# First loads of a fused S5 and GELU-MLP kernel on one core: fewer x transposes, bulk loads in one queue, parameter rows in one transpose

## The chip, the cores and the metric

The kernel runs on one core of a Trainium2 chip. The metric is the device time of one execution in microseconds (us), lower is better. Executions of the same program are compared in rounds on the same chip. Each execution has a time, a span (from the first to the last instruction, 1.3 to 2 us less than the time) and a mean granted clock of TensorE (1.000 is full). An execution is called slow here when it is more than 1.5% above the fastest of its kernel. Verdicts use the others alone, the "fast" ones.

## The reference, cut to what matters

```python
x = A_x                                            # 1 x 2048 x 640, bf16
g = sigmoid((x * gate_w).sum(-1, keepdims=True))
Bu = einsum("bld,pd->blp", x, B_bar)               # complex; B_bar from B_re, B_im, Lambda, log_dt
for t in range(2048): h = Lam_bar * h + Bu[:, t]   # a linear recurrence per state, complex
a = 2 * einsum("blp,dp->bld", h_all, Cmat).real + x * Dskip
b = gelu(x @ w1 + b1) @ w2 + b2                    # 640 -> 1728 -> 640
out = g * a + (1 - g) * b
```

## The kernel before

The kernel cuts the 2048 rows into four tiles of 512. It needs x in two forms: transposed (`xT`, loaded by DMA transposes, which turn the matrix on its way in; 640 on partitions in five slabs of 128, for the matmuls) and natural (`xn`, for the gate and the skip term). TensorE does W1, then B_re and B_im, then W2 and C, tile after tile. VectorE does the recurrence as scans and builds its tables from the parameters first. ScalarE takes results out of PSUM, the memory into which TensorE writes its sums. A small list scheduler in the kernel orders each engine's work from priorities and assumed durations.

TensorE starts with tile 0. It works slab by slab, so that it can start with the first slab of xT and W1:

```python
xtrans(0, [0], 0, 1.27)                 # one DMA transpose for each slab, Sync queue
xtrans(0, [1], 1, 1.27)
w1load(0, "act", -101)
w1load(1, "sp", 2)
for k in range(2, KD):
    xtrans(0, [k], 2 * k - 1, 1.27)
    w1load(k, "sp", 2 * k)
load("w1_r", "sp", ...)                 # the remaining 704 columns of W1, 880 KB
...
for ci, src in enumerate((A_B_re, A_B_im)):
    load_T(f"B{ci}", ..., prio=30 + ci) # two DMA transposes of 640 x 640, Sync queue
xtrans(1, range(KD), 32, 3.4)
load("w2a", "sp", ...); load("w2b", "sp", ...)
xtrans(2, ...); C_re, C_im; xtrans(3, ...)
```

GpSimd's queue loads the rest, as soon as the first matmul on the last slab of W1 is done ("late"):

```python
m1_first()                              # W1, columns 0 to 1023, tile 0
load("b2",  "pool", ..., reads=["late"])
load("dsk", "pool", ..., A_Dskip.partition_broadcast(128), reads=["late"])
load("gwb", "pool", ..., gate_w.partition_broadcast(128), reads=["late"])
xnload(0, "g", ..., reads=["late"])     # natural x tile 0, 640 KB, GpSimd
m1(0, NW)                               # W1, the remaining columns
bproj(0)                                # B_re (25 matmuls), then B_im (25 matmuls)
...
xnload(1, "g", ..., reads=["late"])     # natural x tile 1, 640 KB, GpSimd
```

The parameters (Lambda_re, Lambda_im, log_dt and b1) are loaded as rows and turned into columns by four small TensorE transposes, each result copied by VectorE.

Of the kernel before, what the change touches and what calls it, by code (L numbers as in the profile page):

```python
# [8 lines left out]
FP32 = mybir.dt.float32  # L9
BF16 = mybir.dt.bfloat16  # L10
# [137 lines left out]
class Prog:  # L148
# [8 lines left out]
    def op(self, name, eng, dur, reads, writes, fn, prio=None, lat=0.0, after=()):  # L157
        deps = {}
        for k in reads:
            for w in self.last_w.get(k, ()):  # L160
                deps[w.idx] = w
        for k in writes:
            for w in self.last_w.get(k, ()):
                deps[w.idx] = w
            for r in self.last_r.get(k, ()):
                deps[r.idx] = r
        for a in after:
            deps[a.idx] = a
        deps = list(deps.values())
        E = self.E  # L170

        def run(eg, deps=deps, eng=eng, fn=fn):
            E.wait(eng, *[d.done for d in deps])
            return fn()

        it = self.sch.add(name, eng, dur, deps, run, prio=prio, lat=lat)
        for k in writes:
            self.last_w[k] = [it]
            self.last_r[k] = []
        for k in reads:  # L180
            self.last_r.setdefault(k, []).append(it)
        return it


def bass_gated_mix__ssm_conv_s5__dense_activation_gelu__prompt_kernel(
# [20 lines left out]
    F = B_w1.shape[1]  # L206
    assert S % 512 == 0 and D % 128 == 0 and P == D
    KD = D // 128
    KP = P // 128
# [4 lines left out]
    NF = (F + 127) // 128  # L214
    FL = F - (NF - 1) * 128
# [10 lines left out]
    with ExitStack() as es:  # L226

        def SB(name, shape, dt):
            return es.enter_context(nc.sbuf_tensor(name, list(shape), dt))

        xT = [SB(f"xT_{i}", [128, KD, 512], BF16) for i in range(NQ)]
        xn = [SB(f"xn_{i}", [128, 4, D], BF16) for i in range(2)]
# [4 lines left out]
        Gl = [SB(f"Gl_{i}", [128, NF, 512], BF16) for i in range(2)]  # L237
        dsk = SB("dsk", [128, D], BF16)
        gwb = SB("gwb", [128, D], BF16)
        b1col = SB("b1col", [128, NF], FP32)  # L240
        rows = SB("rows", [KP, 3, 128], BF16)
        b1rows = SB("b1rows", [NF, 128], BF16)
        lcol = SB("lcol", [128, 3, KP], FP32)
        dtb = SB("dtb", [128, KP], BF16)
        acol = SB("acol", [128, KP], FP32)
        thcol = SB("thcol", [128, KP], FP32)
# [5 lines left out]
        ident = SB("ident", [128, 128], BF16)  # L252
# [33 lines left out]
        PS = [es.enter_context(nc.psum_tensor(f"ps{i}", [128, 512], FP32)) for i in range(8)]  # L286
# [13 lines left out]
        op = pr.op  # L300

        def inc(eng, ins):
            return E.inc(eng, ins, eng + "_s")

        def dma_inc(eng, ins, sem):
            SEM(sem)
            E.count.setdefault(sem, 0)
            ins.then_inc(sems[sem], 16)
            E.count[sem] += 16
            return (sem, E.count[sem])  # L310
# [11 lines left out]
        def load(name, eng, sem, dst, src, writes, prio, dur=0.5, lat=2.5, reads=(), **kw):  # L322
            def fn():
                return dma_inc(eng, engines[eng].dma_start(dst, src), sem)  # L324
            return op(name, eng, dur, reads, writes, fn, prio=prio, lat=lat)

        def load_T(name, sem, pairs, writes, prio, dur, lat=3.0):
            def fn():
                t = None
                for dst, src in pairs:  # L330
                    t = dma_inc("sp", nc.sync.dma_start_transpose(dst, src), sem)  # L331
                return t
            return op(name, "sp", dur, (), writes, fn, prio=prio, lat=lat)

        def xnload(q, tag, prio=None, reads=()):
            load(f"xn{q}{tag}", "pool", f"l_xn{q}{tag}", xn[q % 2][:, :, :],
                 x2[q * 512:(q + 1) * 512, :].rearrange("(c p) d -> p c d", p=128),
                 [("xn", q % 2, 0), ("xn", q % 2, 1)], prio, dur=1.0, lat=6.0, reads=reads)

        NW = 8  # L340
        FW = NW * 128
        nmain = (NF - 1) * 128

        def xtrans(q, ks, prio, dur):
            load_T(f"xT{q}_{ks[0]}", f"l_xT{q}_{ks[0]}", [(xT[q][:, ks[0]:ks[-1] + 1, :], x2[q * 512:(q + 1) * 512, ks[0] * 128:(ks[-1] + 1) * 128])],
                   [("xT", q, k) for k in ks], prio, dur)

        def w1load(k, eng, prio):
            load(f"w1_{k}", eng, f"l_w1{k}", W1sb[:, k, 0:FW], B_w1[k * 128:(k + 1) * 128, 0:FW], [("w1", k)], prio=prio, lat=2.6)

        xtrans(0, [0], 0, 1.27)
        xtrans(0, [1], 1, 1.27)
        w1load(0, "act", -101)
        w1load(1, "sp", 2)
        for k in range(2, KD):
            xtrans(0, [k], 2 * k - 1, 1.27)
            w1load(k, "sp", 2 * k)
        load("w1_r", "sp", "l_w1r", W1sb[:, :, FW:F], B_w1[:, FW:F].rearrange("(k p) f -> p k f", p=128), [("w1", "r")], prio=20, lat=5.0)

        def f_b1z():  # L360
            return inc("pool", nc.gpsimd.memset(b1rows[:, :], 0.0))

        op("b1z", "pool", 0.2, (), ["b1a", "b1b0", "b1b1"], f_b1z, prio=-50)
        for i, (nm, src) in enumerate((("lre", A_Lambda_re), ("lim", A_Lambda_im), ("ldt", A_log_dt))):
            load(nm, "act", "l_" + nm, rows[:, i, :], src.rearrange("(k p) -> k p", p=128), [("rows", i)], prio=-100 + i, dur=0.45)
        load("b1a", "act", "l_b1a", b1rows[0:NF - 1, :], B_b1[0:nmain].rearrange("(j p) -> j p", p=128), ["b1a"], prio=-97, dur=0.4)
        for i in range(2):
            load(f"b1b{i}", "act", f"l_b1b{i}", b1rows[NF - 1:NF, 64 * i:64 * i + FL], B_b1[nmain:F].rearrange("(j p) -> j p", j=1), [f"b1b{i}"], prio=-96, dur=0.4)


        def f_iota():
            inc("pool", nc.gpsimd.iota(io_i[:, :], pattern=[[1, 128]], base=0, channel_multiplier=-1))
# [33 lines left out]

        XT = {q: [("xT", q, k) for k in range(KD)] for q in range(NQ)}

        psC = PS[7][:, :].bitcast(BF16)

        def f_cols():
            t = None
            for i in range(3):
                t = nc.tensor.transpose(psC[:, i * 8:i * 8 + KP], rows[:, i, :], ident[0:KP, 0:KP])
            return inc("pe", t)

        op("cols", "pe", 0.3, [("rows", 0), ("rows", 1), ("rows", 2), "ident"], [("bank", 7)], f_cols, prio=7.5)

        def f_cols1():
            return inc("dve", nc.vector.tensor_copy(out=lcol[:, :, :], in_=psC[:, 0:24].rearrange("p (a k) -> p a k", a=3)[:, :, 0:KP]))  # L420

        op("cols1", "dve", 0.2, [("bank", 7)], ["lcol"], f_cols1, prio=-1000)
        psD = PS[7][:, :].bitcast(BF16)[:, 64:64 + NF]

        def f_colb():
            return inc("pe", nc.tensor.transpose(psD, b1rows[:, :], ident[0:NF, 0:NF]))

        op("colb", "pe", 0.1, ["b1a", "b1b0", "b1b1", "ident"], [("bank", 7)], f_colb, prio=7.6)

        def f_colb1():  # L430
            return inc("dve", nc.vector.tensor_copy(out=b1col[:, :], in_=psD))

        op("colb1", "dve", 0.2, [("bank", 7)], ["b1col"], f_colb1, prio=-1000)

        def f_dt():
            return inc("act", nc.scalar.activation(dtb[:, :], lcol[:, 2, :], ACT.Exp))
# [123 lines left out]
        for ci, src in enumerate((A_B_re, A_B_im)):  # L560
            load_T(f"B{ci}", f"l_B{ci}", [(BT[:, ci, :, :], src)], [("BT", ci)], prio=30 + ci, dur=4.1)
        xtrans(1, range(KD), 32, 3.4)
        load("w2a", "sp", "l_w2a", W2sb[:, 0:NF - 1, :], B_w2[0:nmain, :].rearrange("(j p) d -> p j d", p=128), ["w2a"], prio=33, lat=8.0)
        load("w2b", "sp", "l_w2b", W2sb[0:FL, NF - 1, :], B_w2[nmain:F, :], ["w2b"], prio=34, lat=4.0)
        xtrans(2, range(KD), 35, 3.4)
        for ci, src in enumerate((A_C_re, A_C_im)):
            load_T(f"C{ci}", f"l_C{ci}", [(CT[:, ci, :, :], src)], [("CT", ci)], prio=36 + ci, dur=4.1)
        xtrans(3, range(KD), 38, 3.4)

        ctr = {"bank": 0, "pe": 0}  # L570

# [259 lines left out]

        m1_first()
        load("b2", "pool", "l_b2", W2sb[64:65, NF - 1, :], B_b2.rearrange("(o n) -> o n", o=1), ["b2"], prio=-30, dur=1.0, reads=["late"])
        load("dsk", "pool", "l_dsk", dsk[:, :], A_Dskip.partition_broadcast(128), ["dsk"], prio=-29, dur=1.0, reads=["late"])
        load("gwb", "pool", "l_gwb", gwb[:, :], gate_w.partition_broadcast(128), ["gwb"], prio=-28, dur=1.0, reads=["late"])

        xnload(0, "g", prio=-27, reads=["late"])
        m1(0, NW)
        bproj(0)
        ssm(0)  # L840
# [3 lines left out]
        ssm(1)  # L844
        bproj(1)
        ssm(2)
        xnload(1, "g", prio=-26, reads=["late"])
        gates(1)
        outs(0)
        for q in range(2, NQ):  # L850
            ssm(2 * q - 1)
            bproj(q)
            ssm(2 * q)
            m1(q)
            if q % 2 == 1:
                m1_tail(q - 1)
            xnload(q, "g")
            gates(q)
            outs(q - 1)
        ssm(2 * NQ - 1)  # L860
# [61 lines left out]
```

## Time and profile before

| | before |
|---|---|
| median of the three first runs | 218.72 us (218.46 to 219.18) |
| the execution that was profiled: time, span | 222.17 us, 220.8 us |
| its granted clock | 0.992 |
| TensorE (PE) busy | 213.0 us, 96% of the span |
| VectorE (DVE), ScalarE (ACT) busy | 189.5 us, 99.3 us |

The page of the profile of before. The first line after the heading gives busy time and share of each engine. Below, each digit is one fortieth of the span (5.5 us), in tenths; PEclk is the granted clock of TensorE.

```profile
span 220.8 us, 3207 instructions
## 1 busy us (share of the span) xinstructions
PE 213.0 (96%) x1260; PEld 122.1 (55%) x1260; DVE 189.5 (86%) x263; ACT 99.3 (45%) x169; POOL 5.5 (2%) x15
...
PE   7999759999999999999999999999999999999995
...
PEclk9999969999999999999999999999999999999999
DMA  5999999993000041000000004000000000000000
```

TensorE has one dip, in slices 5 and 6 (22 to 33 us), and in slice 6 its clock is low as well. Everything after is full: only the start can give time.

The timeline of before around that dip. Columns: start, duration, engine, line, operation, output and input, count, and in brackets the idle time before with what ended it. SPq and POOL lines are DMA issues; the duration there is that of the issue, not of the transfer.

```profile
10.23 5.97 SPq L331 DMA_TRANSPOSE BT<-in_A_B_re_dram  x1
...
14.44 0.57 POOL L324 DMA_DIRECT2D dsk<-in_A_Dskip_dram  x1
...
14.99 0.54 POOL L324 DMA_DIRECT2D gwb<-in_gate_w_dram  x1
...
15.52 1.51 POOL L324 DMA_DIRECT2D xn<-in_A_x_dram  x2
...
16.24 10.30 SPq L331 DMA_TRANSPOSE BT<-in_A_B_im_dram  x1
...
20.79 5.56 PE L667 MATMUL ps<-xT,BT 128*128 128x512 bf16 x25
...
30.01 6.98 PE L667 MATMUL ps<-xT,BT 128*128 128x512 bf16 x25 [3.66 <-DMA BT<-in_A_B_im_dram]
```

TensorE ends its 25 matmuls on B_re at 26.35 us and stands 3.66 us until B_im has landed. The next 25 take 6.98 instead of 5.56 us. Between 14.4 and 17 us GpSimd has issued 1.6 MB that run beside B. The same stretch in windows of 2 us (TensorE busy, instructions, granted clock, DMA share, GB/s) shows the clock falling to half:

```profile
core 0: us, PE busy (x), PEclk, DMA share, GB/s
26.00:28.00 2.00, 0.35 (x2) 1.00 1.17 227
28.00:30.00 2.00, 0.00 (x0) 0.87 0.95 112
30.00:32.00 2.00, 1.99 (x5) 0.50 1.20 235
32.00:34.00 2.00, 2.00 (x8) 0.77 0.91 302
```

The DMA view of before gives the time from issue to landing (last number). B and C are the same size, 640 x 640:

```profile
BT<-in_A_B_re_dram SPq DMA_TRANSPOSE x1, 10.2
...
BT<-in_A_B_im_dram SPq DMA_TRANSPOSE x1, 13.7
CT<-in_A_C_re_dram SPq DMA_TRANSPOSE x1, 6.3
CT<-in_A_C_im_dram SPq DMA_TRANSPOSE x1, 6.8
```

### The profile page before, as it was taken

How to read it: one execution, taken by the hardware profiler on the slowest of the kernel's cores; microseconds unless marked ns; L12 is line 12 of the kernel's file. 1: busy time of each engine (PE TensorE's matmuls, PEld its weight loads, DVE VectorE, ACT ScalarE, POOL GpSimd, SP SyncE). 2: the span in 40 equal slices, each digit the busy share in tenths (PEclk: the TensorE clock that was granted, in tenths of full speed). 3: DMA queues.
4: the chain of work that ended last, by engine and by line, in shares of the span. 5: the costliest groups of instructions: out<-in, count | busy, mean ns of one | idle time of the engine just before them, and what ended most of it. 6: DMA issues, size and time to landing. Idle time of an engine off the chain costs nothing.

```text
span 220.8 us, 3207 instructions
## 1 busy us (share of the span) xinstructions
PE 213.0 (96%) x1260; PEld 122.1 (55%) x1260; DVE 189.5 (86%) x263; ACT 99.3 (45%) x169; POOL 5.5 (2%) x15
## 2 busy tenths in 40 slices
PE   7999759999999999999999999999999999999995
PEld 2334324444467777444457777544446777777773
DVE  3699992999997999999999999599999999997312
ACT  2568515667543323456653233455664232323330
POOL 1050000000000010000000010000000000000000
PEclk9999969999999999999999999999999999999999
DMA  5999999993000041000000004000000000000000
GB/s 110 213 294 299 184 193 368 244 189 83 0 0 3 30 131 47 33 0 0 0 3 0 30 33 150 30 0 3 0 0 3 0 30 30 33 30 30 33 30 30
DMA packets 29785, 16.09 MB, mean 73 GB/s; under 512 B 24012, under 2 KB 28556, under 8 KB 29772
## 3 DMA queue, kind: packets, MB, share of 16 engines
q1 hardware_dynamic: 28864, 12.68, 23.7%
q0 software_dynamic: 704, 2.95, 4.7%
q10 hardware_dynamic: 204, 0.27, 0.5%
q8 instruction: 10, 0.16, 0.3%
q14 instruction: 3, 0.02, 0.0%
HBM read 7.38 MB, written 2.62 MB: 45 GB/s over the span
## 4 chain that ended last, share of the span: by engine, by line
PE 85%; SPq 7%; DMA 6%; issue 0%; DVE 0%
PE ps L742 28%; PE ps L769 20%; PE ps L628 19%; PE ps L667 18%; DMA BT<-in_A_B_im_dram 6%; SPq L331 5%; SPq L324 1%; PE ps L646 1%; DVE osb L802 0%
## 5 line engine op out<-in xcount | busy, mean ns | idle before, releaser
L742 PE MATMUL ps<-W2sb,Gl 128*128 128x320 bf16 x448 | 63.6, 299 | 0.0
L742 PEld LDWEIGHTS ps<-W2sb,Gl 128*128 128x128 bf16 x448 | 43.8, 98 | 17.5
L667 PE MATMUL ps<-xT,BT 128*128 128x512 bf16 x200 | 45.4, 387 | 3.7 <-DMA BT<-in_A_B_im_dram 3.7
L628 PE MATMUL ps<-xT,W1sb 128*128 128x512 bf16 x220 | 48.1, 379 | 0.4 <-DMA W1sb<-in_B_w_dram 0.4
L769 PE MATMUL ps<-CT,H 128*128 128x320 bf16 x320 | 46.3, 299 | 0.0
L707 DVE TENSOR_TENSOR_SCAN W<-atab,V 128x1280 bf16<-128x1280 f32 x16 | 44.3, 2811 | 0.3
L769 PEld LDWEIGHTS ps<-CT,H 128*128 128x128 bf16 x320 | 31.2, 98 | 12.6 <-issue 0.4
L635 ACT ACTIVATE Gl<-ps,b1col 128x512 bf16<-128x512 f32 x44 | 30.0, 692 | 15.8 <-PE ps L628 15.8
L750 ACT ACTIVATE E<-ps,g1col 128x320 bf16<-128x320 f32 x32 | 16.9, 528 | 43.7 <-PE ps L742 43.7
L628 PEld LDWEIGHTS ps<-xT,W1sb 128*128 128x128 bf16 x220 | 21.5, 98 | 26.6 <-DMA W1sb<-in_B_w_dram 0.9
L667 PEld LDWEIGHTS ps<-xT,BT 128*128 128x128 bf16 x200 | 19.7, 100 | 28.4 <-DMA BT<-in_A_B_im_dram 4.1
L676 ACT ACTIVATE U<-ps 128x512 bf16<-128x512 f32 x40 | 23.9, 597 | 23.5 <-PE ps L667 23.5
L780 ACT ACTIVATE E<-ps,gcol 128x320 bf16<-128x320 f32 x30 | 15.8, 528 | 24.2 <-PE ps L769 24.1
L476 DVE TENSOR_TENSOR osb<-xg,E 128x640 bf16<-128x640 bf16 x15 | 7.3, 488 | 10.5 <-ACT E L780 9.6
L476 DVE TENSOR_TENSOR V<-mr,U 128x2560 bf16<-128x2560 bf16 x8 | 11.9, 1489 | 4.5 <-ACT U L676 4.3
L788 DVE SCALAR_TENSOR_TENSOR xg<-xn,gcol,dsk 128x640 bf16<-128x640 bf16 x16 | 13.9, 884 | 0.4
L585 DVE SCALAR_TENSOR_TENSOR scr<-xn,gwb 128x640 bf16<-128x640 bf16 x16 | 13.2, 823 | 0.4
L476 DVE TENSOR_TENSOR H<-H,V 128x1280 bf16<-128x1280 bf16 x16 | 12.5, 822 | 0.3
L476 DVE TENSOR_TENSOR V<-V,W 128x1280 bf16<-128x1280 bf16 x16 | 12.5, 822 | 0.3
L476 DVE TENSOR_TENSOR H<-c,W 128x2560 bf16<-128x2560 bf16 x8 | 11.9, 1489 | 0.1
L476 DVE TENSOR_TENSOR V<-s,W 128x2560 bf16<-128x2560 bf16 x8 | 11.9, 1485 | 0.0
L476 DVE TENSOR_TENSOR W<-mi,U 128x2560 bf16<-128x2560 bf16 x8 | 11.9, 1485 | 0.0
(82 smaller groups left out, 86.9 us busy)
## 6 DMA issues: line engine op xcount, KB each, us to landing
xn<-in_A_x_dram POOLq DMA_DIRECT2D x4, 640.0 KB, 5.4
out_dram<-osb SPq DMA_DIRECT2D x15, 160.0 KB, 1.8
W2sb<-in_B_w_dram SPq DMA_DIRECT2D x1, 2080.0 KB, 8.7
W1sb<-in_B_w_dram SPq DMA_DIRECT2D x4, 256.0 KB, 3.3
W1sb<-in_B_w_dram SPq DMA_DIRECT2D x1, 880.0 KB, 5.6
W1sb<-in_B_w_dram ACTq DMA_DIRECT2D x1, 256.0 KB, 2.8
dsk<-in_A_Dskip_dram POOLq DMA_DIRECT2D x1, 160.0 KB, 4.2
gwb<-in_gate_w_dram POOLq DMA_DIRECT2D x1, 160.0 KB, 4.7
```

The costliest lines, as they stand in the source:

```text
L476: return inc("dve", nc.vector.tensor_tensor(out=o, in0=a, in1=b, op=o_))
L585: t = inc("dve", nc.vector.scalar_tensor_tensor(out=scr[:, :], in0=xn[q % 2][:, c, :], scalar=1.0, in1=gwb[:, :], op0=ALU.mult, op1=ALU.mu ...
L628: t = nc.tensor.matmul(PS[bank][:, :], W1sb[:, k, jf * 128:(jf + 1) * 128], xT[q][:, k, :], start=(k == 0), stop=(k == KD - 1))
L635: return inc("act", nc.scalar.activation(Gl[q % 2][:, jf, :], PS[bank][:, :], ACT.Gelu_apprx_tanh, bias=b1col[:, jf:jf + 1]))
L667: t = nc.tensor.matmul(PS[bank][:, :], BT[:, ci, kd, k * 128:(k + 1) * 128], xT[q][:, kd, :], start=(kd == 0), stop=(kd == KD - 1))
L676: return inc("act", nc.scalar.activation(dst, src, ACT.Copy, scale=1.0 if ci == 0 else -1.0))
L707: t = inc("dve", nc.vector.tensor_tensor_scan(out=g[:, ci, :], data0=a, data1=v[:, ci, :], initial=0.0, op0=ALU.mult, op1=ALU.add))
L742: t = nc.tensor.matmul(PS[bank][:, 0:HALF], Gl[q % 2][0:n, jf, t4 * 128:(t4 + 1) * 128], W2sb[0:n, jf, cols], start=(jf == 0), stop=(jf == ...
L750: return inc("act", nc.scalar.activation(E1[c % NE][:, cols], PS[bank][:, 0:HALF], ACT.Copy, scale=g1col[:, c:c + 1]))
L769: t = nc.tensor.matmul(PS[bank][:, 0:HALF], H[b % NHB][:, ci, k, s * 128:(s + 1) * 128], CT[:, ci, k, cols], start=(i == 0), stop=(i == 2 ...
L780: return inc("act", nc.scalar.activation(E2[c % NE][:, cols], PS[bank][:, 0:HALF], ACT.Copy, scale=gcol[:, c:c + 1]))
L788: return inc("dve", nc.vector.scalar_tensor_tensor(out=xg[c % 2][:, :], in0=xn[q % 2][:, c % 4, :], scalar=gcol[:, c:c + 1], in1=dsk[:, :] ...
```

## The change

The intent is to feed TensorE without a gap at the start. There are three parts. **Slabs:** xT of tile 0 comes in three transposes of 1, 2 and 2 slabs. **Queue:** the two first natural x tiles, the gate row and Dskip leave GpSimd's queue and go into the Sync queue, behind B and xT of tile 1, and xT of tiles 2 and 3 goes last. **Parameters:** all parameter rows sit in one 128 x 128 tile and are turned by one transpose and one copy.

```diff
+        w1load(0, "act", -101)
         xtrans(0, [0], 0, 1.27)
-        xtrans(0, [1], 1, 1.27)
-        w1load(0, "act", -101)
+        xtrans(0, [1, 2], 1, 1.27)
         w1load(1, "sp", 2)
-        for k in range(2, KD):
-            xtrans(0, [k], 2 * k - 1, 1.27)
-            w1load(k, "sp", 2 * k)
+        w1load(2, "sp", 3)
+        xtrans(0, [3, 4], 4, 1.27)
+        w1load(3, "sp", 5)
+        w1load(4, "sp", 6)
 ... (parameters)
-            for i in range(3):
-                t = nc.tensor.transpose(psC[:, i * 8:i * 8 + KP], rows[:, i, :], ident[0:KP, 0:KP])
+            return inc("pe", nc.tensor.transpose(psC, rows[:, :], ident[:, :]))
 ... (a second transpose and copy for b1 are dropped)
         xtrans(1, range(KD), 32, 3.4)
+        load("gwb", "sp", ..., prio=32.2)
+        xnload(0, "sp", prio=32.4)
         load("w2a", "sp", ...)
         load("w2b", "sp", ...)
-        xtrans(2, range(KD), 35, 3.4)
         ... (C_re, C_im)
-        xtrans(3, range(KD), 38, 3.4)
+        load("dsk", "sp", ..., prio=38)
+        xnload(1, "sp", prio=38.2)
+        xtrans(2, range(KD), 39, 3.4)
+        xtrans(3, range(KD), 40, 3.4)
 ...
-        load("dsk", "pool", ..., reads=["late"])
-        load("gwb", "pool", ..., reads=["late"])
-        xnload(0, "g", prio=-27, reads=["late"])
 ...
-        xnload(1, "g", prio=-26, reads=["late"])
```

The order of instructions on TensorE and ScalarE is otherwise the same.

More of the change, by code (lines that the diff above doesn't have):

```diff
@@ L239, in bass_gated_mix__ssm_conv_s5__dense_activation_gelu__prompt_kernel @@
         gwb = SB("gwb", [128, D], BF16)
-        b1col = SB("b1col", [128, NF], FP32)
-        rows = SB("rows", [KP, 3, 128], BF16)
-        b1rows = SB("b1rows", [NF, 128], BF16)
-        lcol = SB("lcol", [128, 3, KP], FP32)
+        rows = SB("rows", [128, 128], BF16)
+        cols = SB("cols", [128, 3 * KP + NF], FP32)
+        lcol = cols[:, 0:3 * KP].rearrange("p (a k) -> p a k", a=3)
+        b1col = cols[:, 3 * KP:3 * KP + NF]
         dtb = SB("dtb", [128, KP], BF16)
@@ L333, in load_T, with xnload @@
             return op(name, "sp", dur, (), writes, fn, prio=prio, lat=lat)
-        def xnload(q, tag, prio=None, reads=()):
-            load(f"xn{q}{tag}", "pool", f"l_xn{q}{tag}", xn[q % 2][:, :, :],
+        def xnload(q, eng, prio=None):
+            load(f"xn{q}", eng, f"l_xn{q}", xn[q % 2][:, :, :],
                  x2[q * 512:(q + 1) * 512, :].rearrange("(c p) d -> p c d", p=128),
-                 [("xn", q % 2, 0), ("xn", q % 2, 1)], prio, dur=1.0, lat=6.0, reads=reads)
+                 [("xn", q % 2, 0), ("xn", q % 2, 1)], prio, dur=1.0, lat=6.0)
         NW = 8
@@ L349, in w1load, with f_rz @@
             load(f"w1_{k}", eng, f"l_w1{k}", W1sb[:, k, 0:FW], B_w1[k * 128:(k + 1) * 128, 0:FW], [("w1", k)], prio=prio, lat=2.6)
+        w1load(0, "act", -101)
         xtrans(0, [0], 0, 1.27)
-        xtrans(0, [1], 1, 1.27)
-        w1load(0, "act", -101)
+        xtrans(0, [1, 2], 1, 1.27)
         w1load(1, "sp", 2)
-        for k in range(2, KD):
-            xtrans(0, [k], 2 * k - 1, 1.27)
-            w1load(k, "sp", 2 * k)
+        w1load(2, "sp", 3)
+        xtrans(0, [3, 4], 4, 1.27)
+        w1load(3, "sp", 5)
+        w1load(4, "sp", 6)
         load("w1_r", "sp", "l_w1r", W1sb[:, :, FW:F], B_w1[:, FW:F].rearrange("(k p) f -> p k f", p=128), [("w1", "r")], prio=20, lat=5.0)
-        def f_b1z():
-            return inc("pool", nc.gpsimd.memset(b1rows[:, :], 0.0))
-        op("b1z", "pool", 0.2, (), ["b1a", "b1b0", "b1b1"], f_b1z, prio=-50)
-        for i, (nm, src) in enumerate((("lre", A_Lambda_re), ("lim", A_Lambda_im), ("ldt", A_log_dt))):
-            load(nm, "act", "l_" + nm, rows[:, i, :], src.rearrange("(k p) -> k p", p=128), [("rows", i)], prio=-100 + i, dur=0.45)
-        load("b1a", "act", "l_b1a", b1rows[0:NF - 1, :], B_b1[0:nmain].rearrange("(j p) -> j p", p=128), ["b1a"], prio=-97, dur=0.4)
-        for i in range(2):
-            load(f"b1b{i}", "act", f"l_b1b{i}", b1rows[NF - 1:NF, 64 * i:64 * i + FL], B_b1[nmain:F].rearrange("(j p) -> j p", j=1), [f"b1b{i}"], prio=-96, dur=0.4)
+        ROWS = {"lre": (0, A_Lambda_re), "lim": (KP, A_Lambda_im), "ldt": (2 * KP, A_log_dt), "b1a": (3 * KP, B_b1[0:nmain])}
+        RT = 3 * KP + NF - 1
+        def f_rz():
+            return inc("pool", nc.gpsimd.memset(rows[:, :], 0.0))
+        op("rz", "pool", 0.2, (), list(ROWS) + ["b1b"], f_rz, prio=-90)
+        for i, (nm, (r0, src)) in enumerate(ROWS.items()):
+            src = src.rearrange("(k p) -> k p", p=128)
+            load(nm, "act", "l_" + nm, rows[r0:r0 + src.shape[0], :], src, [nm], prio=-100 + i, dur=0.4)
+        load("b1b", "act", "l_b1b", rows[RT:RT + 1, :].rearrange("o (a p) -> o a p", a=2),
+             B_b1[nmain:F].rearrange("(o p) -> o p", o=1).unsqueeze(1).broadcast_to([1, 2, FL]), ["b1b"], prio=-96, dur=0.4)
         def f_iota():
@@ L407, in bass_gated_mix__ssm_conv_s5__dense_activation_gelu__prompt_kernel @@
         XT = {q: [("xT", q, k) for k in range(KD)] for q in range(NQ)}
-        psC = PS[7][:, :].bitcast(BF16)
+        psC = PS[7][:, :].bitcast(BF16)[:, 0:128]
         def f_cols():
-            t = None
-            for i in range(3):
-                t = nc.tensor.transpose(psC[:, i * 8:i * 8 + KP], rows[:, i, :], ident[0:KP, 0:KP])
-            return inc("pe", t)
-        op("cols", "pe", 0.3, [("rows", 0), ("rows", 1), ("rows", 2), "ident"], [("bank", 7)], f_cols, prio=7.5)
-        def f_cols1():
-            return inc("dve", nc.vector.tensor_copy(out=lcol[:, :, :], in_=psC[:, 0:24].rearrange("p (a k) -> p a k", a=3)[:, :, 0:KP]))
-        op("cols1", "dve", 0.2, [("bank", 7)], ["lcol"], f_cols1, prio=-1000)
-        psD = PS[7][:, :].bitcast(BF16)[:, 64:64 + NF]
-        def f_colb():
-            return inc("pe", nc.tensor.transpose(psD, b1rows[:, :], ident[0:NF, 0:NF]))
-        op("colb", "pe", 0.1, ["b1a", "b1b0", "b1b1", "ident"], [("bank", 7)], f_colb, prio=7.6)
-        def f_colb1():
-            return inc("dve", nc.vector.tensor_copy(out=b1col[:, :], in_=psD))
-        op("colb1", "dve", 0.2, [("bank", 7)], ["b1col"], f_colb1, prio=-1000)
+            return inc("pe", nc.tensor.transpose(psC, rows[:, :], ident[:, :]))
+        op("cols", "pe", 0.3, list(ROWS) + ["b1b", "ident"], [("bank", 7)], f_cols, prio=7.5)
+        def f_cols1():
+            return inc("dve", nc.vector.tensor_copy(out=cols[:, :], in_=psC[:, 0:RT + 1]))
+        op("cols1", "dve", 0.2, [("bank", 7)], ["lcol", "b1col"], f_cols1, prio=-1000)
         def f_dt():
@@ L562, in bass_gated_mix__ssm_conv_s5__dense_activation_gelu__prompt_kernel @@
         xtrans(1, range(KD), 32, 3.4)
+        load("gwb", "sp", "l_gwb", gwb[:, :], gate_w.partition_broadcast(128), ["gwb"], prio=32.2)
+        xnload(0, "sp", prio=32.4)
         load("w2a", "sp", "l_w2a", W2sb[:, 0:NF - 1, :], B_w2[0:nmain, :].rearrange("(j p) d -> p j d", p=128), ["w2a"], prio=33, lat=8.0)
         load("w2b", "sp", "l_w2b", W2sb[0:FL, NF - 1, :], B_w2[nmain:F, :], ["w2b"], prio=34, lat=4.0)
-        xtrans(2, range(KD), 35, 3.4)
         for ci, src in enumerate((A_C_re, A_C_im)):
             load_T(f"C{ci}", f"l_C{ci}", [(CT[:, ci, :, :], src)], [("CT", ci)], prio=36 + ci, dur=4.1)
-        xtrans(3, range(KD), 38, 3.4)
+        load("dsk", "sp", "l_dsk", dsk[:, :], A_Dskip.partition_broadcast(128), ["dsk"], prio=38)
+        xnload(1, "sp", prio=38.2)
+        xtrans(2, range(KD), 39, 3.4)
+        xtrans(3, range(KD), 40, 3.4)
         ctr = {"bank": 0, "pe": 0}
@@ L833, in bass_gated_mix__ssm_conv_s5__dense_activation_gelu__prompt_kernel @@
         load("b2", "pool", "l_b2", W2sb[64:65, NF - 1, :], B_b2.rearrange("(o n) -> o n", o=1), ["b2"], prio=-30, dur=1.0, reads=["late"])
-        load("dsk", "pool", "l_dsk", dsk[:, :], A_Dskip.partition_broadcast(128), ["dsk"], prio=-29, dur=1.0, reads=["late"])
-        load("gwb", "pool", "l_gwb", gwb[:, :], gate_w.partition_broadcast(128), ["gwb"], prio=-28, dur=1.0, reads=["late"])
-        xnload(0, "g", prio=-27, reads=["late"])
         m1(0, NW)
@@ L856, in bass_gated_mix__ssm_conv_s5__dense_activation_gelu__prompt_kernel @@
                 m1_tail(q - 1)
-            xnload(q, "g")
+            xnload(q, "pool")
             gates(q)
```

## The prediction

> **What bounds the kernel now.** The page gives TensorE 213.0 of 220.8 us busy (VectorE 189.5, ScalarE 99.3); the chain of waits runs on TensorE unbroken from 30.01 to 218.56 us. So time can only come out of the part before 30 us. There the timeline shows:
> - first matmul on data at 5.00 us, the 40 of the first stage (five slabs) ended at 14.99 us, with about 0.3 us of holes around the parameter transposes (6.9 and 7.5 us) and a few tenths at slab changes;
> - 0.39 us waiting for the rest of W1;
> - 25 matmuls on B_re, then 3.66 us waiting for B_im, TensorE's longest wait: issued at 16.24, landed at 29.96 us, 13.7 us later;
> - the 25 of B_im take 6.98 us against 5.56 us for B_re's: 1.4 us lost to a cold clock (granted clock 0.50 in 30 to 32 us). The Trainium skill, "TensorE: Matmul & The Clock Gate", Part 1, says that an idle window of about 3.4 us halves the clock; this trace agrees, with 3.66 us.
>
> **Why B_im is late.** GpSimd's queue issues b2, Dskip, the gate row and two x tiles (1.6 MB) between 13.8 and 17 us; the DMA share reads 1.0 to 1.5 in 12 to 22 us. The two C transposes, of the same size, took 6.3 and 6.8 us beside xT and W2 only; B took 10.2 and 13.7 us. The Trainium skill, "DMA: Bandwidth & Descriptors", "Issuing engines are not separate DMA queues", says that all issuers share 16 engines; these durations agree.
>
> **What the change does.**
> - Those 1.6 MB now follow B and xT1 in the Sync queue. At the 250 to 350 GB/s of the slices there, that is 4.6 to 6.4 us of DMA work (estimate).
> - One slab costs 1.12 to 1.31 us of issue, five cost 3.33, so about 1.7 us for two (estimate). B_re is issued at about 8.6 instead of 10.2 us.
> - Together B_im should land at 22 to 25 us; it is needed at 25 to 26 us: no wait, no cold clock. xT1 lands by 28 us, needed at about 31 us.
> - Four small TensorE transposes become one: 0.2 to 0.4 us less. Against it, W1's second slab is issued at about 3.8 instead of 3.34 us and slab 1 lands with slab 2: a stall of 0 to 0.4 us. Net gain 0.2 us.
> - VectorE builds tables until 33.4 us in both; its first block then follows at once instead of waiting 4.3 us for U. It falls about 1 us behind TensorE; the tightest place, H of block 1, has 3.5 us of slack (ready 76.5, needed 79.99 us).
> - W2, C, Dskip, xT2, xT3 move less than 10 us and stay in time.
>
> **Sum.** 3.66 + 1.4 + 0.2 + about 0.3 for the W1 wait and slab changes = 5.5 us, all on the critical path: 218.72 - 5.5 = 213.2 us, 2.5% faster. Range 212.0 to 215.2 us. Faster by over 2% (under 214.3 us): 0.82; within 2%: 0.17; slower: 0.01.
>
> **Signs.** Right: no wait of TensorE for B_im; granted clock 1.0 through 26 to 34 us; B_im lands before 25 us, within 10 us of issue; VectorE's first block at 33.5 us. Wrong: a wait for B_im remains, or another comes up (slab 1 or 3, xT1, W2, the gate's E copies, H of block 1).
>
> **What would make it wrong.** If B is slow because of the transposes and W1 rather than GpSimd's loads, 1 to 3 us of the wait stay. If the two-slab transposes land late, TensorE stalls in its first stage and may go cold.

## The result, and the profile after

The changed kernel takes 216.57 us (216.26 to 217.02, 4 runs); before in the same comparison 218.95 us, with one execution at 224.93 us. The ratio is 0.990 with a 95% interval of 0.987 to 0.993: faster by 1%, so within 2%. Ratios here are the mean time of one kernel's fast runs over that of the other's in the same rounds, so they are not quite the ratio of the medians quoted. The measured time lies above the range that I had given (212.0 to 215.2 us).

The page after:

```profile
span 215.1 us, 3184 instructions
## 1 busy us (share of the span) xinstructions
PE 210.9 (98%) x1247; PEld 122.0 (57%) x1257; DVE 189.3 (88%) x262; ACT 99.0 (46%) x169; POOL 3.0 (1%) x11
...
PE   7999999999999999999999999999999999999995
...
PEclk9999999999999999999999999999999999999999
DMA  6999799994000230100000022000000000000001
```

The dip and the low clock are gone. The timeline after (the lines answer to those of before; L660 is the B projection, and one of its 50 matmul records is missing in the trace):

```profile
7.48 6.51 SPq L331 DMA_TRANSPOSE BT<-in_A_B_re_dram  x1
...
14.03 3.85 SPq L331 DMA_TRANSPOSE BT<-in_A_B_im_dram  x1
...
20.32 10.96 PE L660 MATMUL ps<-xT,BT 128*128 128x512 bf16 x49
...
33.70 1.49 DVE L465 TENSOR_TENSOR V<-mr,U 128x2560 bf16<-128x2560 bf16 x1
```

B_re is issued 2.75 us earlier, B_im 2.2 us earlier, and TensorE goes through B_re and B_im without a stop. VectorE's first block starts at 33.70 us. The windows after:

```profile
core 0: us, PE busy (x), PEclk, DMA share, GB/s
26.00:28.00 2.00, 2.00 (x10) 1.00 1.01 342
28.00:30.00 2.00, 2.00 (x11) 1.00 1.05 381
30.00:32.00 2.00, 2.00 (x11) 1.00 1.06 396
```

The DMA view after:

```profile
BT<-in_A_B_re_dram SPq DMA_TRANSPOSE x1, 9.4
...
BT<-in_A_B_im_dram SPq DMA_TRANSPOSE x1, 6.4
CT<-in_A_C_re_dram SPq DMA_TRANSPOSE x1, 10.4
```

B_im lands 6.4 instead of 13.7 us after its issue, at 14.03 + 6.4 = 20.4 us. C_re now takes 10.4 instead of 6.3 us. It is issued at 27.56 us, while W2 is still in flight (issued at 23.05 us, landed about 11 us later); before, W2 had landed at 38.8 us, just before C_re was issued at 39.18 us. Nothing waits for it.

All signs that I had named for "right" are there. And the two profiled spans differ by 220.8 - 215.1 = 5.7 us, where I had predicted 5.5. Still the time fell by 2.15 us only (218.72 - 216.57). The profiled execution after took 216.53 us, like its median. So about 3.4 us are missing, and the first suspect is the side of before: its profiled execution was not like the ones that make its median.

### The profile page after: what moved, and what is told of

Its sections match the earlier page's. It is cut to its first block, busy times and chain, and to the rows that moved or that the text cites. A ratio compares the mean times of both kernels' runs of the same rounds, so it can differ in the third digit from the quotient of the medians.

```text
span 215.1 us, 3184 instructions
## 1 busy us (share of the span) xinstructions
PE 210.9 (98%) x1247; PEld 122.0 (57%) x1257; DVE 189.3 (88%) x262; ACT 99.0 (46%) x169; POOL 3.0 (1%) x11
## 4 chain that ended last, share of the span: by engine, by line
PE 98%; DVE 0%; issue 0%
PE ps L735 28%; PE ps L621 22%; PE ps L762 20%; PE ps L660 20%; PE ps L601 5%; PE ps L399 2%; PE ps L639 1%; DVE osb L795 0%; DVE wz L392 0%; PE ps L415 0%
## 5 line engine op out<-in xcount | busy, mean ns | idle before, releaser
L621 PE MATMUL ps<-xT,W1sb 128*128 128x512 bf16 x214 | 47.3, 379 | 0.3
L660 PE MATMUL ps<-xT,BT 128*128 128x512 bf16 x196 | 43.1, 379 | 0.3 <-PE ps L639 0.2
L628 ACT ACTIVATE Gl<-ps,cols 128x512 bf16<-128x512 f32 x44 | 29.8, 694 | 15.5 <-PE ps L621 15.5
L660 PEld LDWEIGHTS ps<-xT,BT 128*128 128x128 bf16 x200 | 19.5, 98 | 23.5 <-issue 0.4
L465 DVE TENSOR_TENSOR V<-mr,U 128x2560 bf16<-128x2560 bf16 x8 | 11.9, 1489 | 0.2
L465 DVE TENSOR_TENSOR H<-c,W 128x2560 bf16<-128x2560 bf16 x8 | 11.9, 1490 | 0.1
L465 DVE TENSOR_TENSOR V<-s,W 128x2560 bf16<-128x2560 bf16 x8 | 11.9, 1485 | 0.0
L465 DVE TENSOR_TENSOR W<-mi,U 128x2560 bf16<-128x2560 bf16 x8 | 11.9, 1484 | 0.0
## 6 DMA issues: line engine op xcount, KB each, us to landing
W2sb<-in_B_w_dram SPq DMA_DIRECT2D x1, 2080.0 KB, 11.1
```

Source lines behind the costliest of these rows:

```text
L465: return inc("dve", nc.vector.tensor_tensor(out=o, in0=a, in1=b, op=o_))
L621: t = nc.tensor.matmul(PS[bank][:, :], W1sb[:, k, jf * 128:(jf + 1) * 128], xT[q][:, k, :], start=(k == 0), stop=(k == KD - 1))
L628: return inc("act", nc.scalar.activation(Gl[q % 2][:, jf, :], PS[bank][:, :], ACT.Gelu_apprx_tanh, bias=b1col[:, jf:jf + 1]))
L660: t = nc.tensor.matmul(PS[bank][:, :], BT[:, ci, kd, k * 128:(k + 1) * 128], xT[q][:, kd, :], start=(kd == 0), stop=(kd == KD - 1))
```

## The experiments

Theory A: the wait for B_im differs from execution to execution of the kernel before, and the profiled one was long; its usual wait is 1 to 2.5 us, without the fall of the clock. Theory B: the wait and the cold clock are always there, and the change loses 3 us elsewhere. On the cause of the wait there is a second pair: GpSimd's loads beside B (as predicted), or, rival C, the late issue of B behind W1 and five transposes.

Spans, and how many executions had full clock (1.000):

| run | edit, against | span at full clock, us | executions at full clock | ratio to before (95%) |
|---|---|---|---|---|
| before, in all runs of the experiments | none | 216.6 to 218.2, median 217.0 | 23 of 49 | 1 |
| change | all three parts | 214.8 to 215.6 | 4 of 4 | 0.990 (0.987 to 0.993) |
| e2 | queue part alone, before | 214.9 to 215.4 | 6 of 6 | 0.994 (0.992 to 0.996) |
| e3 | slab part alone, before | 215.3 to 216.6 | 5 of 6 | 0.996 (0.992 to 0.999) |
| e4 | parameter part alone, before | 216.3 to 217.5 | 3 of 6 | 1.003 (0.995 to 1.010) |
| e6 | GpSimd's loads later, before | 214.9 to 215.7 | 6 of 6 | 0.992 (0.990 to 0.994) |
| e7 | queue part undone, change | 214.8 to 216.9 | 6 of 6 | 0.994 (0.990 to 0.998) |
| e8 | slab part undone, change | 215.0 to 215.7 | 6 of 6 | 0.992 (0.990 to 0.993) |
| e11 | filler matmuls, before | 218.2 to 220.0 | 4 of 6 | 1.009 (1.004 to 1.014) |

What follows rests on spans, clocks and waits. The spans are the better thing to compare here: the ratios of e2 and e8 differ only because other executions of before counted as fast in their rounds. All outputs were correct. The experiments were made on three chips, each with before in the same rounds.

### e1: the kernel before again

No edit.

> The kernel before, unchanged, to see how its executions differ. Theory A (the profiled execution of before was an unlucky one: its own time was 222.2 us, 3.5 us above the median of 218.7): most executions have spans of 217 to 218 us with a granted clock of 0.995 or more, TensorE's wait for B_im is 1 to 2.5 us in them, and a few executions of 221 us and more have a clock of 0.992 or less. Theory B (the 3.7 us wait and the cold clock are in every execution, and the change loses 3 us elsewhere): the spans are all near 220.8 minus at most 1 us with a clock of 0.992, and this profile shows a wait of 3.5 us or more again.

Three of eight executions had full clock, with spans of 216.6, 217.7 and 218.2 us; the others had 0.992 or 0.985 and spans of 220.8 to 224.5 us. The twelve runs of before in the same rounds split likewise (five and seven). So there are two groups with nothing between 218.2 and 220.0 us, and the profile that I predicted from (220.8 us, clock 0.992) belongs to the second. Theory B, one wait for all, falls. What theory A got wrong is how rare the second group is: it is about half. This run's own profile was of that group (wait 4.72 us), so the first group's wait was still unseen. The three runs that make the median of 218.72 us have no clock on record, but their times (218.46 to 219.18 us) lie among those of the 23 executions at full clock (217.98 to 219.54 us).

### e5, e9 and e10: looking for a profile of before at full clock

No edit; one look each.

> The kernel before again, for a profile of one of its executions at full clock. So far its executions at clock 1.000 have spans of 216.6 to 218.2 us, those at 0.992 or 0.985 have 220.0 to 224.5 us, and both profiles seen are of the second kind. Theory A: in an execution at clock 1.000 TensorE waits 1.0 to 2.5 us for B_im, which lands 10 to 12.5 us after its issue, and no matmul after the wait is at half clock. Theory B: the wait is 3 us or more there too, and the time is found again elsewhere.

> The kernel before once more, for a profile at clock 1.000 (span 216.6 to 218.2 us). All variants without a wait for B_im have spans of 215.1 to 215.4 us. Theory A: a profile at clock 1.000 shows a wait of 1.2 to 2.2 us for B_im, and span minus wait is 215 us. A profile at 0.992 would show 3.5 to 5 us again, and tells nothing new.

> As the one before it: a further chance of a profile of the kernel before at clock 1.000, with a wait of 1.2 to 2.2 us under theory A.

e5 missed: clock 0.992, wait 3.9 us, span 221.2 us. e9 had full clock and a span of 216.7 us. Its timeline, with the same work as that of before above:

```profile
16.19 7.60 SPq L331 DMA_TRANSPOSE BT<-in_A_B_im_dram  x1
...
27.34 5.57 PE L667 MATMUL ps<-xT,BT 128*128 128x512 bf16 x25 [1.03 <-DMA BT<-in_A_B_im_dram]
```

Its windows:

```profile
core 0: us, PE busy (x), PEclk, DMA share, GB/s
26.00:28.00 2.00, 0.97 (x6) 1.00 1.05 163
28.00:30.00 2.00, 2.00 (x11) 1.00 1.04 202
```

B_im is issued at the same time as in the first profile and lands 11.1 us later instead of 13.7. TensorE waits 1.03 us instead of 3.66 us, the clock stays at 1.00, and the 25 matmuls on B_im take 5.57 us instead of 6.98 us. With 0.44 us of waiting for the rest of W1, the two waits are 1.47 us, and 216.7 - 1.47 = 215.2 us. That lies within the 214.8 to 215.7 us of the change, e2, e6 and e8, which do not wait for B_im. The expected wait (1.2 to 2.2 us) was slightly too high.

e10, also at full clock (span 217.8 us), lost its time in another place: 1.24 us for the rest of W1, 0.55 us for B_re, 0.22 us for B_im, and two holes of 0.7 us together in the first stage. So even at full clock before does not have one wait but several that vary, 1.5 to 2.7 us in the two profiles. The expectation, one wait of 1.2 us or more for B_im, missed here.

### e2, e3 and e4: one part of the change at a time

e2 takes the queue part of the diff above onto the kernel before, e3 the slab part, e4 the parameter part; the edits are those blocks of the diff, unaltered.

> Only the queue part of the change: the two first x tiles, the gate row and Dskip go from GpSimd's queue to the Sync queue behind B and xT1. Theory A with GpSimd's loads as what delays B_im: B_im lands before 25.5 us, wait under 0.3 us, time 216.5 to 217.2 us, steady within 0.8 us. Rival C (B_im is late because it is issued late, behind W1 and five single transposes): a wait of over 1 us for B_im stays, time 218 to 219 us.

> Only the transposes of 1, 2 and 2 slabs (with the new order of W1's slabs); GpSimd's loads stay. B_re should be issued at about 7.5 instead of 10.2 us. Theory A with GpSimd's loads as the cause: B_im still meets them, is at most 1.5 us earlier, and the time is 217.4 to 218.7 us with some executions over 220 us. Rival C: B_im lands 2.5 us earlier, wait under 0.3 us, time 216.5 to 217.2 us.

> Only the parameter rows in one transpose. Under A and C alike: TensorE comes 0.1 to 0.4 us earlier to its wait for B_im and waits that much longer; time within 0.3 us of before (218.4 to 219.0 us). If it is 0.5 us or more faster, the parameters are on the path in a way that I do not see.

e2: 216.93 us, all six executions at full clock and within 0.6 us of one another; B_im landed 6.3 us after its issue, and TensorE went through all 50 matmuls on B without a stop:

```profile
20.61 10.96 PE L671 MATMUL ps<-xT,BT 128*128 128x512 bf16 x50
```

By span it is the whole gain to within 0.2 us (medians of 215.3 and 215.15 us).

e3: 217.3 us (216.9 to 218.4), and one execution of 227.3 us at clock 0.977. In the profile GpSimd's loads still stretch B_im to 11.9 us, but B_im was issued at 14.23 us, so it lands at 26.1 us, just when it is needed, and TensorE goes on without a stop:

```profile
14.23 3.64 SPq L331 DMA_TRANSPOSE BT<-in_A_B_im_dram  x1
...
20.78 10.96 PE L668 MATMUL ps<-xT,BT 128*128 128x512 bf16 x50
```

So rival C is right in part: issuing B earlier removes most of the wait as well. It leaves no margin.

e4: nothing gained. Its fast runs include one at clock 0.992 (220.75 us), which widens the interval and lifts the ratio. Its profile (slow) shows a wait of 4.18 us. Where two parts each remove the same wait, they don't add: 215.3 us of span with the queue part alone, 215.2 with everything.

### e6: GpSimd's loads later, in their own queue

```diff
-        load("dsk", "pool", ..., reads=["late"])      # gwb and xnload(0) likewise
         m1(0, NW)
         bproj(0)
+        load("dsk", "pool", ..., reads=["late2"])     # gwb and xnload(0), xnload(1) likewise
```

"late2" is written by the last B_im matmul of tile 0.

> The kernel before with one edit: GpSimd's loads of Dskip, the gate row and the first two x tiles stay in GpSimd's queue but start only after the last B_im matmul of the first tile. If those loads beside B are the cause of the wait and of its spread: B_im lands 6 to 8 us after its issue, no wait over 0.3 us, clock 1.000 in all executions, 216.6 to 217.3 us, as the queue part alone (216.9). If it is the queue that they go through, or the issue time of B, that counts: a wait of 1 us or more stays, with executions above 220 us.

216.82 us, six of six executions at full clock, no wait for B_im. The DMA view of e6:

```profile
BT<-in_A_B_re_dram SPq DMA_TRANSPOSE x1, 8.7
...
BT<-in_A_B_im_dram SPq DMA_TRANSPOSE x1, 6.3
CT<-in_A_C_re_dram SPq DMA_TRANSPOSE x1, 16.5
CT<-in_A_C_im_dram SPq DMA_TRANSPOSE x1, 13.6
```

And its timeline:

```profile
20.64 10.96 PE L667 MATMUL ps<-xT,BT 128*128 128x512 bf16 x49
```

Here B is issued as late as before (10.16 and 16.07 us), through the same queues, with the same five transposes. Only the overlap in time with GpSimd's loads is taken away, and B_im takes 6.3 us instead of 11.0 to 14.8 us. So the overlap is what stretches B_im, and without it the waits and the spread are gone. The stretch moved with the loads: from 31.92 us on they are issued beside the C transposes, which now take 16.5 and 13.6 us instead of 6.3 and 6.8. Whether GpSimd's queue (here) or the Sync queue (e2) carries the later loads made no difference that shows. This is what the Trainium skill states ("DMA: Bandwidth & Descriptors", "Issuing engines are not separate DMA queues": DMAs of all issuers run on the same 16 engines and interleave).

### e7 and e8: one part undone

e7 is the changed kernel with the queue block of the diff reverted; e8 is the changed kernel with the slab block reverted.

> The changed kernel with the queue part undone (slabs and parameters stay changed; the loads go through GpSimd beside B again). B is issued 2.5 us earlier than before, so B_im lands at about 26 us, near the time it is needed: 216.5 to 217.3 us at clock 1.000, but now and then an execution above 220 us, since the margin is under 1 us. If GpSimd's loads were the only cause, it would be as before: 218 us and half of the executions above 220.

> The changed kernel with the slab part undone (five single transposes). B_re is issued at about 10 us, B_im lands at about 22.5 us, 3 us before it is needed: no wait, all executions at clock 1.000, 216.3 to 217.0 us, within 0.4 us of the whole change. If the earlier issue of B is needed, a wait for B_im of over 0.5 us shows.

e8: 216.59 us, as the whole change. With the loads out of the way, the three transposes instead of five add nothing that shows in the medians of the spans (215.2 and 215.15 us). Its profile, the longest of the six (215.7 us), has no wait for B_im, but 1.56 us before the matmuls on the rest of W1, whose weights waited for that load; the first B matmul starts at 20.98 us, 0.66 us later than after the whole change. e7: four executions with spans of 214.8 to 215.3 us, two with 216.8 and 216.9 us. The profile fell on one of these two:

```profile
14.15 6.46 SPq L331 DMA_TRANSPOSE BT<-in_A_B_im_dram  x1
...
27.61 5.34 PE L656 MATMUL ps<-xT,BT 128*128 128x512 bf16 x24 [1.85 <-DMA BT<-in_A_B_im_dram]
```

It is a clean case of a wait without a fall of the clock: 1.85 us of wait, 1.7 us more span than its neighbours. I had expected executions above 220 us "now and then"; there were none in six here, and one in six in e3.

### e11: matmuls on zeros in the empty time

```diff
+                    if (q, ci, k) == (0, 1, 0):
+                        def f_fill(bank=bank):
+                            for _ in range(10):
+                                t = nc.tensor.matmul(PS[bank][:, :], wz[:, 0:128], wz[:, :], start=True, stop=True)
+                            return inc("pe", t)
+                        op("fill", "pe", 0.0, ["wz"], [("bank", bank)], f_fill, prio=pe_prio())
```

The next matmul into that bank starts a new sum, so the result stays correct. The scheduler shifted a few instructions of the other engines by it.

> The kernel before with ten matmuls on zeros (512 columns, about 2.2 us at full clock), whose result is thrown away, between the last B_re matmul and the wait for B_im: TensorE's empty time is cut by 2.2 us and the landing of B_im is not touched. Theory A (executions above 220 us are those whose empty time lasts long enough for the clock to fall): none or few executions are left with a clock under 0.995, the wait that remains is 1.3 to 2.5 us in what would have been slow executions, their spans fall to 217.5 to 219.5 us, and the fast ones stay within 0.7 us of 216.6 to 217.5. Rival E (the slow executions are slow for another reason, and the clock falls whatever TensorE does): clocks of 0.992 and 0.985 and spans above 220 us stay as frequent as before, about half.

This is mixed. Four of six executions had full clock, three of them with spans of 219.1 to 220.0 us, where before has no execution at full clock at all: there, it seems, the fall of the clock was saved and the wait remained; none of these was profiled. But two executions still fell (0.992), none was as fast as 217.5 us, and the kernel is slower than before. The zeros themselves cost time where B_im comes early: they ran for 2.32 us in the trace, so e9's execution with them would have a span of about 216.7 + 2.32 - 1.03 = 218.0 us (estimate). With six executions against 23 of 49, the frequency alone doesn't refute rival E. The other runs speak against it: if the clock fell whatever TensorE does, about half of the 22 executions of the change, e2, e6 and e8 should have fallen, and none did. Nor do GpSimd's loads beside B lower the clock without a long wait: in e3 and e7, where they stay but B is issued earlier, 11 of 12 executions have full clock. The profile was of one that fell:

```profile
31.02 7.26 PE L667 MATMUL ps<-xT,BT 128*128 128x512 bf16 x25 [2.56 <-DMA BT<-in_A_B_im_dram]
```

2.56 us of empty time were enough. The params-only profile (e4) shows the same without zeros in front: its last B_re matmul ended before 26.0 us, and the clock fell at 28.6 us:

```profile
25.50:26.00 0.50, 0.49 (x3) 1.00 0.98 242
26.00:26.50 0.50, 0.00 (x0) 1.00 1.37 169
...
28.50:29.00 0.50, 0.00 (x0) 0.61 1.24 115
```

## Why the prediction was wrong

The step that failed is the line "**Sum.** 3.66 + 1.4 + 0.2 + about 0.3 ... 218.72 - 5.5 = 213.2 us". The 3.66 and the 1.4 were read from an execution that took 222.17 us, and taken off the median of executions that took 218.7 us. From the time of the execution that they belong to, the same sum gives 222.17 - 5.5 = 216.7 us; measured were 216.57. The mechanism held between the two profiles; its size did not hold for the usual execution. At full clock before has a median span of 217.0 us, the change one of 215.15 us: 1.85 us, where 5.5 were expected.

| term | predicted | measured in before at full clock (e9, if not said otherwise) |
|---|---|---|
| wait for B_im | 3.66 us | 1.03 us |
| cold clock after it | 1.4 us | 0 |
| W1 wait and slab changes | 0.3 us | 0.44 us (W1 wait) |
| parameters, first stage | 0.2 us | about 0 (see below) |
| sum | 5.5 us | 1.5 us; span 216.7 to 215.1 us is 1.6 us |

In e10 the waits are others, with only 0.22 us for B_im, but again no cold clock: 2.7 us in all.

Point by point:

- **TensorE bounds the kernel, and the time can only come from the start.** Right. The chain of waits after the change stays on TensorE to the end.
- **B_im is late because of GpSimd's loads.** Right, shown by e6. It was not the only way out: e3 shows that an earlier issue also does, with no margin. The comparison with C in the prediction was weaker than it looked, since W2 had landed before C_re was issued.
- **B_im lands at 22 to 25 us.** It landed at 20.4 us. B_re was issued at 7.48 us, not 8.6: in the timeline a two-slab transpose took 1.22 us to issue, not 1.7, no more than one slab.
- **Net gain of 0.2 us in the first stage.** Not there. The first 40 matmuls end at 15.09 us after and at 14.99 us before. B's first matmul still starts 0.47 us earlier (20.32 against 20.79 us), mostly because the wait of 0.39 us for the rest of W1 is gone; that the sum's 0.2 and 0.3 us come near to this is luck. The parameter part changes nothing that shows in e4's wide interval, the slab part at most 0.2 us of median span beyond the wait (e8).
- **VectorE falls 1 us behind without harm.** Right: first block at 33.70 us (33.5 predicted), and no new wait of TensorE.
- **Within the list of what could make it wrong** there was nothing of this kind. I asked whether the wait would go, not whether the usual execution had it.

What stays open is why the same instructions let B_im land 11.0 to 11.1 us after its issue in some executions (e10, e9) and 13.7 to 14.8 us in others. In the windows of 20 to 24 us the slow profile of e1 moves 277 and 82 GB/s, e9 moves 355 and 238. That the overlap with GpSimd's loads is needed for it is shown (e2, e6, e8: none of 18 executions below full clock); how the engines share it differently is not.

The fast-run verdict is 1%. Over all executions the kernel before had a mean of 222.0 us (49 executions), since half of them fall below full clock. The profiles of such executions (first, e1, e5; 220.8 to 222.1 us) show the longer wait and the cold matmuls; 17 of the 26 were longer than any that was profiled, and what they lost is not shown. The changed kernel had no such execution in its four runs, nor had e2, e6 or e8. This steadiness is not counted in the 1%, and four runs are too few to call it proven for the changed kernel itself.

## What to carry to other kernels

Before you subtract a wait from a time, check that the profiled execution is one of those that make up that time: compare its time, span and granted clock with those of the timed runs, and if they differ, take the saving off the profiled execution's own time or profile again. A transfer that is needed soon should not share the DMA engines with bulk loads that are needed much later; moving those in time was enough here, in GpSimd's queue (e6) as in the Sync queue (e2). When two parts of a change remove the same wait, their gains don't add, and the one that leaves margin is the one to keep.

## What the Trainium skill lacked or had wrong

- "TensorE: Matmul & The Clock Gate", Part 1, gives an idle window of about 3.4 us, free-running, for the fall to half clock. The falls seen here came 2.6 us (e4), 2.6 us (e11), 3.1 us (first profile), 4.2 us (e1) and 4.2 us (e5) after the last matmul before the wait, read from windows of 0.1 us (in e5 and e11 the next matmuls had just begun). In a wait of 1.85 us (e7) the clock stayed at 1.00. A window of 3.4 us that must be idle throughout cannot end sooner than 3.4 us after the last matmul, wherever it starts; three of the five falls came sooner, the first profile's among them, which the prediction had called an agreement. So a wait under 3.4 us is not safe; how much work a window may hold and still lead to a fall is not shown here.
- "DMA: Bandwidth & Descriptors", "Issuing engines are not separate DMA queues", says that DMAs of different issuers interleave, but gives no size. Here a 640 x 640 transpose took 6.3 us (e2, e6) without GpSimd's 1.6 MB beside it and 11.0 to 14.8 us with it (B_im, profiles of before), different in each execution.
- No page read says to check whether the profiled execution is one of the usual ones: before had spans of 216.6 to 218.2 us and of 220.0 to 228.0 us, about half each.
- "DMA: Bandwidth & Descriptors", "DMA Transpose (X-bar)", gives no issue time by size: a transpose of one slab (512 x 128) took 1.1 to 1.6 us of the Sync queue's time here, one of two slabs 1.22 us (after the change, at 4.64 us), one of five slabs 2.9 to 3.7 us where it was not held up.
